# A one-core FFT filter with a maxout MLP: start-up work spread over ScalarE, GpSimd, VectorE and SyncE in another way

## The chip, the core and the metric

The kernel runs on one core of one Trainium2 chip. The metric is device microseconds of that core from the start to the end of one execution. The core has five engines that run side by side, each with its own instruction queue that is worked off in order: TensorE (PE in the profile; its weight loads are PEld), VectorE (DVE), ScalarE (ACT), GpSimd (POOL) and SyncE (SP), which here only issues DMAs. GpSimd issues DMAs too. Engines wait for each other through semaphores.

## What is computed

Per batch entry (8 of them, 3072 positions, 256 channels) a real FFT along the positions is multiplied by a filter and transformed back; every position then passes a maxout MLP.

```python
X = np.fft.rfft(x, axis=1)                       # x: (8, 3072, 256)
F = (filt_r + 1j * filt_i)[None, :, :]           # (1, 1537, 256)
y = np.fft.irfft(X * F, n=x.shape[1], axis=1)
h1, h2 = y @ w1, y @ w2                          # w1, w2: (256, 1024)
out = np.maximum(h1, h2) @ w_out                 # w_out: (1024, 256)
```

Inputs and output are float32; the kernel multiplies in bfloat16.

## The kernel before, in words

**Transforms as matmuls.** 3072 is split into 96 x 32. S1 (`s1t`, L507, for batch entry 0) multiplies x, 96 rows at a time, by the 96 x 96 sine and cosine table C1; x comes in eight chunks c of four m each. Its two results per chunk (dc = 0, 1) are evicted from PSUM to `at2` by ScalarE, or by VectorE where L514 says so. `t1` (L519) transposes `at2` into `bt`, in six parts. S2 (`s2`, L383) multiplies `bt` by the table U, the filter products `pq` (`product`, L392) come from VectorE and GpSimd, S3 (`s3t`, L530) goes back with the tables VP and VQ, which are U transposed on TensorE (`table_v`, `put_v`), and S4 (`s4`, L434) ends the transform with G1. The MLP (`moe_h`, L454, and `moe_o`, L475) uses max(h1, h2) = h2 + max(h1 - h2, 0): it needs Wd = w1 - w2 (`prep_wd`, on GpSimd, four parts), M = w2 w_out (`prep_t`, `prep_m`) and Wo = w_out. Batch entries 1 to 7 go through other functions (`f1`, `s1`, `visit`), which a plan interleaves with the MLP of the entry before; that part is long and is not touched.

**The tables** are computed at the start. C1 (`table_c`, L184): arguments on VectorE, then a sine on ScalarE, for which it loads its sine table (`ACT_TABLE_LOAD`). U (`tables_u`, L208): small columns on VectorE, four rows `t2` on ScalarE (L231), then for each half h the arguments `ua` on VectorE (L240 to L251), and a sine per half (`sines_u`).

**x of entry 0.** Chunks 0 and 1 are loaded as float32 by SyncE (L93) and cast to bfloat16 by ScalarE (`cast_x0`, L96); chunks 2 to 7 are loaded by GpSimd's DMAs, which cast on the way (L88). TensorE takes the chunks in the order 0, 2, 1, 3, 4, 5, 6, 7, with two matmuls on constants (`spin`) between them.

**The filter.** `load_f` (L119) brings the filter with GpSimd's DMAs, first half h = 0 (frequencies w 0 to 7), then h = 1 (w 8 to 11), each with g = 0, 1 (partitions 0 to 31 and 64 to 95) and real and imaginary part: four quarters per half, each of two or three DMAs. `double_f` (L135) copies a quarter to the 32 partitions behind it: half 0 by VectorE (L139), half 1 by SyncE's DMA (L141). `fix_f` mends one row.

**Order.** The program is written in the order in which each engine gets its work (manual schedule). On GpSimd: loads of x and small tables, `load_f`, four products, `prep_wd` with the loads of entry 1's x (L88) and of Wo (L300) between its parts. On SyncE: chunks 0 and 1, one filter row, the doublings of half 1, then w1 and w2 (L293, L294). On VectorE: the arguments of C1 and U, the S1 evictions of c = 6, 7, then by turns doublings and `bt` copies, then products. A DMA on either queue reuses one of eight semaphores, so it waits until the eighth before it has landed.

Of the kernel before, what the change touches and what calls it, by code (L numbers as in the profile page):

```python
# [17 lines left out]
NP = 96  # L18
# [8 lines left out]
def kernel(  # L27
# [55 lines left out]
    def load_x(b, c, n):  # L83
        for k in range(c, c + n):
            xb[b, k] = x_tile(b, k)[0:NP]
        src = x[b].rearrange("(p m) d -> p m d", m=NM)
        m0 = 4 * (c % 2)
        G.dma_start(out=xb[b][0:NP, m0:m0 + 4 * n], in_=src[:, 4 * c:4 * c + 4 * n, :])  # L88
# [4 lines left out]
        nc.sync.dma_start(out=XF[c][0:NP].rearrange("p a b d -> p (a b) d"),  # L93
                          in_=x[0].rearrange("(p m) d -> p m d", m=NM)[:, 4 * c:4 * c + 4, :])

    def cast_x0(c):  # L96
        S.activation(xb[0, c], XF[c][0:NP].rearrange("p a b d -> p (a b) d"), AF.Copy)  # L97

    def load_xf(b, c):
        src = x[b].rearrange("(h p m) d -> p h m d", h=2, m=NM)  # L100
# [34 lines left out]
    def double_f(h, g, ri, engine):  # L135
        w0, w1 = WP[h]
        o_, i_ = F[64 * g + 32:64 * g + 64, ri, w0:w1], F[64 * g:64 * g + 32, ri, w0:w1]
        if engine is V:
            V.tensor_copy(o_, i_)  # L139
        else:  # L140
            nc.sync.dma_start(out=o_, in_=i_)  # L141
# [31 lines left out]
    G.iota(cid, pattern=[[1, 128]], base=0, channel_multiplier=0, allow_small_or_imprecise_dtypes=True)  # L173
    for c in range(5, 8):
        load_x(0, c, 1)
    for q in range(2):
        G.memset(hv[:, q], 1.0)
        for r in (0, 32):
            G.memset(hv[r:r + 1, q], 0.5 * (1 - q))
# [4 lines left out]
    def table_c():  # L184
        p96 = init.tile([128, 1], FP32)
        V.tensor_scalar(p96, pid, 1.0 / 96.0, None, OP.mult)
        uc = init.tile([NP, 48, 2], FP32)
        rc = init.tile([NP, 48, 2], FP32)
        kf = kc.rearrange("p w g s -> p (w g s)")
        V.tensor_scalar(uc[:, :, 0], kf, p96[0:NP], 0.25, OP.mult, OP.add)  # L190
        V.tensor_scalar(uc[:, :, 1], kf, p96[0:NP], None, OP.mult)
        V.tensor_scalar(uc[:, 0:1, 1], pid[0:NP], 0.5, 0.25, OP.mult, OP.add)
        V.tensor_scalar(rc, uc, RND, RND, OP.add, OP.subtract)
        V.tensor_tensor(uc, uc, rc, OP.subtract)
        cast_x0(0)
        S.activation(C1, uc.rearrange("p k r -> p (k r)"), AF.Sin, bias=zero[0:NP], scale=TWO_PI)
        cast_x0(1)

    def table_ct():
        G.memset(CT, 0.0)  # L200
# [7 lines left out]
    def tables_u():  # L208
        def col(name):
            return init.tile([128, 1], FP32, name=name)  # L210

        pr, pm, rr, mm, a_, b_, base, nbase = (col("col%d" % i) for i in range(8))
        V.tensor_scalar(pr, pid, 64.0, None, OP.is_ge)
        V.tensor_scalar(pm, pr, -64.0, pid, OP.mult, OP.add)
        V.tensor_scalar(rr, pm, 32.0, None, OP.is_ge)
        V.tensor_scalar(mm, rr, -32.0, pm, OP.mult, OP.add)
        V.tensor_scalar(a_, mm, 1.0 / 3072.0, None, OP.mult)
        V.tensor_scalar(b_, mm, 1.0 / 32.0, None, OP.mult)
        V.tensor_tensor(base, pr, a_, OP.mult)
        of = init.tile([128, 2, 2], FP32)  # L220
        os_ = init.tile([128, 2], FP32)
        for c in range(2):
            V.tensor_scalar(of[:, c, 0:1], rr, 0.25, 0.25 + 0.25 * c, OP.mult, OP.add)
            V.tensor_scalar(of[:, c, 1:2], rr, -0.25, 0.25 + 0.25 * c, OP.mult, OP.add)
        V.tensor_scalar(of[:, :, 1], of[:, :, 1], b_, None, OP.add)
        for c in range(2):
            V.tensor_scalar(os_[32:64, c:c + 1], mm[32:64], 1.0 / 64.0, 0.25 + 0.25 * c, OP.mult, OP.add)
        t2 = init.tile([128, 2, 2, 16], FP32)
        for c in range(2):
            for s in range(2):  # L230
                S.activation(t2[:, c, s], jb, AF.Identity, bias=of[:, c, s:s + 1], scale=b_)  # L231
        t1 = init.tile([128, 2, NU], FP32)
        V.tensor_scalar(t1[:, 0], kap.rearrange("p w g -> p (w g)"), a_, base, OP.mult, OP.add)
        V.tensor_scalar(t1[:, 1], t1[:, 0], -1.0, None, OP.mult)
        uv = ua.rearrange("p u c s j -> p u (c s j)")
        for h in range(2):
            us = slice(NW * h, NW * h + NW)
            for c in range(2):
                for s in range(2):
                    V.tensor_tensor(ua[:, us, c, s],  # L240
                                    t1[:, s, us].rearrange("p (u o) -> p u o", o=1).to_broadcast([128, NW, 16]),
                                    t2[:, c, s].rearrange("p (o j) -> p o j", o=1).to_broadcast([128, NW, 16]),
                                    OP.add)
            if h == 0:
                V.tensor_scalar(ua[0:32, 0, 1, 0, 0:1], mm[0:32], 0.5, 0.25, OP.mult, OP.add)
                for c in range(2):
                    V.tensor_scalar(ua[32:64, 0, c, 1], jb[32:64], b_[32:64], os_[32:64, c:c + 1], OP.mult, OP.add)
                V.memset(ua[0:32, 0, :, 1], 0.0)
                V.memset(ua[32:64, 0, :, 0], 0.0)
            V.tensor_scalar(ru, uv[:, us], RND, RND, OP.add, OP.subtract)  # L250
            V.tensor_tensor(uv[:, us], uv[:, us], ru, OP.subtract)  # L251

    def sines_u(h):
        uv = ua.rearrange("p u c s j -> p u (c s j)")
# [7 lines left out]
    def table_v(h, q):  # L262
        pool, tag = (pso, "po") if h else (ps, "ps")
        pv = [pool.tile([128, 6, 64], FP32, tag=tag, name="pv%d" % s) for s in range(2)]
        for i in range(6):
            for g in range(2):
                for s in range(2):
                    rows = slice(64 * s, 64 * s + 64)
                    u = 2 * (6 * h + i) + g
                    if q == 0:  # L270
                        TE.matmul(pv[s][64 * g:64 * g + 64, i], U[rows, u], I128[rows, rows], start=True, stop=True)
                    else:
                        TE.matmul(pv[s][64 * g:64 * g + 32, i], U[rows, u, 32:64], I128[rows, rows],
                                  start=True, stop=True)
                        TE.matmul(pv[s][64 * g + 32:64 * g + 64, i], U[rows, u, 0:32], NI[rows, rows],
                                  start=True, stop=True)
        return pv

    def put_v(h, q, pv):
        for s in range(2):  # L280
            i0 = 1 if h == 0 and s == 0 else 0
            tab = VQ if q else VP
            if i0:
                S.activation(tab[:, 0, 0], pv[0][:, 0], AF.Identity, bias=zero, scale=hv[:, q])
            S.activation(tab[:, 6 * h + i0:6 * h + 6, s], pv[s][:, i0:6], AF.Copy)  # L285
# [13 lines left out]
    def load_wo():  # L299
        G.dma_start(out=Wo, in_=moe_w_out.rearrange("(c p) j -> p c j", p=128))  # L300

    def prep_wd(h, engine):
        js = slice(256 * h, 256 * h + 256)
        engine.tensor_tensor(Wd[:, :, js], w1f[:, :, js], w2f[:, :, js], OP.subtract)
# [202 lines left out]
    def s1t(c):  # L507
        for dc in range(2):
            pa = ps.tile([128, 4, 96], FP32, tag="ps", name="pa")
            for m in range(4):  # L510
                TE.matmul(pa[:, m], xb[0, c][:, m, 128 * dc:128 * dc + 128], C1, start=True, stop=True)
            o_ = at2[:, dc].rearrange("p u q m -> p (u q) m")[:, :, 4 * c:4 * c + 4]
            i_ = pa.rearrange("p m q -> p q m")
            if dc == 1 and c >= 6:  # L514
                V.tensor_copy(o_, i_)
            else:
                S.activation(o_, i_, AF.Copy)

    def t1(n, engine):  # L519
        pb = ps.tile([128, 4, D], BF16, tag="ps", name="pb")  # L520
        for i in range(4):
            for dc in range(2):
                TE.transpose(pb[:, i, 128 * dc:128 * dc + 128],
                             at2[:, dc, 4 * n + i].rearrange("p q m -> p (q m)"), I128)
        if engine is S:
            S.activation(bt[0][:, 4 * n:4 * n + 4], pb, AF.Copy)  # L526
        else:
            V.tensor_copy(bt[0][:, 4 * n:4 * n + 4], pb)
# [45 lines left out]
    table_c()  # L574
    V.tensor_scalar(I128, cid, pid, None, OP.is_equal)
    V.tensor_scalar(NI, cid, pid, -1.0, OP.is_equal, OP.mult)
    tables_u()
    for g in range(2):
        for ri in range(2):
            double_f(1, g, ri, nc.sync)  # L580
# [9 lines left out]
    sines_u(0)  # L590
    bt[0] = bpool.tile([128, NU, D], BF16, tag="bt", name="bt")
    for n in range(6):
        if n % 2 == 0:
            double_f(0, n // 4, n // 2 % 2, V)
        if n == 0:
            fix_f()
        t1(n, S if n % 2 else V)
    put_v(0, 0, table_v(0, 0))
    double_f(0, 1, 1, V)
    xs = {}  # L600

    def stage_x(v):
# [40 lines left out]
        pqs[v] = products(v)  # L643
    for v in (4, 5):
        s3t(v, pqs[v])
    prep_wd(0, G)
    load_x(1, 2, 2)
    prep_wd(1, G)
    load_x(1, 4, 2)
    load_wo()  # L650
    prep_wd(2, G)
    load_x(1, 6, 2)
    prep_wd(3, G)
# [101 lines left out]
```

## Time and profile before

| | |
|---|---|
| three runs | 507.33, 507.25, 505.11 us; median 507.25 |
| the profiled execution | 506.41 us, span 504.6 us |
| busy: TensorE | 488.9 us, 97% of the span |
| busy: VectorE, ScalarE, GpSimd | 332.4, 311.4, 255.5 us |
| mean granted TensorE clock | 0.99 |

The profile has one execution, with the start of every instruction in us from the start of the span. A timeline row gives start, duration, engine, line of the kernel, operation, what is written from what, the shapes, the count of instructions put together in the row, and in square brackets how long the engine had stood idle and what released it. A chain row gives start, duration, and the engine and line that the end of the program hung on at that moment; "issue" is time in which nothing was waited for that the profile shows. The granted clock is the share of full speed at which TensorE was allowed to run.

### The profile page before, as it was taken

Reading aid. Unit: us, or ns where it says so; the run is one execution under the profiler, and the core shown is the slowest. Engines: PE = TensorE matmul, PEld = TensorE weight load, DVE = VectorE, ACT = ScalarE, POOL = GpSimd, SP = SyncE. Lnnn points to the kernel's source line nnn. Section 1 sums busy time; section 2 is a strip of 40 time slices with the busy share of each in tenths; the row PEclk is TensorE's granted clock in tenths of the full one; section 3 lists DMA queues with packets and bytes.
Section 4 is the critical chain, followed back from the end, with each engine's and each line's share of the span. In section 5 each row is a group of like instructions: output and inputs, shape, how many; then the busy total and the mean of one; then the engine's idle time right before and its main releaser. Section 6 shows DMA issues by size and latency. Waiting matters only on the chain.

```text
span 504.6 us, 13082 instructions
## 1 busy us (share of the span) xinstructions
PE 488.9 (97%) x5300; PEld 362.6 (72%) x5300; DVE 332.4 (66%) x518; ACT 311.4 (62%) x632; POOL 255.5 (51%) x338
## 2 busy tenths in 40 slices
PE   6688999999999999999999999999999999999997
PEld 3455767777777777777777777777777777777775
DVE  6976678557775687557764687557764687554443
ACT  7776377746774586547774676646774465544442
POOL 7694369566663855627654656538632221222220
PEclk8979999999999999999999999999999999999999
DMA  9969789996699658886789659796669336411112
GB/s 190 168 172 189 220 231 299 289 268 210 209 257 280 179 179 245 247 221 200 198 244 259 190 187 256 216 256 185 197 178 248 89 112 162 168 64 64 64 64 84
DMA packets 77966, 97.59 MB, mean 193 GB/s; under 512 B 8017, under 2 KB 54354, under 8 KB 77842
## 3 DMA queue, kind: packets, MB, share of 16 engines
q1 hardware_dynamic: 64866, 67.52, 50.1%
q0 software_dynamic: 13040, 29.24, 19.9%
q8 instruction: 41, 0.67, 0.6%
q14 instruction: 19, 0.16, 0.1%
HBM read 53.87 MB, written 47.19 MB: 200 GB/s over the span
## 4 chain that ended last, share of the span: by engine, by line
PE 88%; DMA 5%; ACT 3%; DVE 2%; POOL 1%; issue 1%; SPq 0%; ACTq 0%; DVEq 0%
PE po L488 33%; PE ph L460 32%; PE po L486 8%; PE pz L411 5%; PE py L440 4%; PE pa L361 2%; PE px L388 2%; DMA Wo<-in_moe_w_out_dram 2%; DMA bt<-ad 1%; DMA XF<-in_x_dram 1%; DMA ad<-at 0%; PE pr L561 0%; ACT bt L526 0%; DVE ua L240 0%; ACT xb L97 0%
## 5 line engine op out<-in xcount | busy, mean ns | idle before, releaser
L488 PE MATMUL po<-Wo,gt 128*128 128x256 bf16 x1536 | 261.0, 273 | 0.6 <-DMA Wo<-in_moe_w_out_dram 0.6
L464 ACT ACTIVATE gt<-ph 128x384 bf16<-128x384 f32 x321 | 157.0, 496 | 147.9 <-PE ph L460 147.3
L473 POOL DMA_DIRECT2D out_dram<-ot x186 | 102.6, 555 | 184.0 <-DVE ot L500 181.1
L488 PEld LDWEIGHTS <-gt 128*128 128x128 bf16 x1536 | 146.6, 98 | 66.5 <-issue 10.7
L462 DVE TENSOR_SCALAR gt<-ph 128x384 bf16<-128x384 f32 x191 | 104.9, 552 | 63.0 <-PE ph L460 61.1
L394 DVE TENSOR_TENSOR pq<-px,F 128x1024 bf16<-128x1024 f32 x91 | 107.1, 1219 | 24.8 <-PE px L388 24.2
L460 PEld LDWEIGHTS <-Wd 128*128 128x128 bf16 x1024 | 96.6, 98 | 12.0 <-issue 0.5
L112 POOL TENSOR_TENSOR xb<-XF 128x512 bf16<-128x512 f32 x48 | 61.2, 1276 | 45.7 <-DMA XF<-in_x_dram 23.6
L500 DVE COPY ot<-po 128x512 f32<-128x512 f32 x95 | 65.1, 685 | 25.3 <-PE po L488 24.1
L113 POOL TENSOR_TENSOR xb<-XF 128x512 bf16<-128x512 f32 x48 | 61.0, 1271 | 0.0
L365 ACT ACTIVATE at<-pa 128x512 bf16<-128x512 f32 x96 | 51.8, 610 | 1.4 <-PE pa L361 1.1
L415 ACT ACTIVATE zt<-pz 128x512 bf16<-128x512 f32 x84 | 45.6, 595 | 11.5 <-PE pz L411 9.2
L440 PE MATMUL py<-G,zr 96*128 96x96 bf16 x512 | 32.7, 206 | 0.2
L440 PEld LDWEIGHTS <-zr 96*128 96x128 bf16 x512 | 28.9, 97 | 2.8 <-DVE zr L564 0.9
L388 PE MATMUL px<-bt,U 64*64 64x256 bf16 x384 | 20.2, 277 | 2.3 <-ACT VQ L285 1.0
L411 PE MATMUL pz<-pq,VP 64*64 64x256 bf16 x336 | 21.9, 281 | 0.0
L411 PE MATMUL pz<-pq,VQ 64*64 64x256 bf16 x336 | 20.9, 269 | 0.0
L361 PE MATMUL pa<-xb,CT 64*64 64x512 bf16 x192 | 19.5, 383 | 0.0
L411 PEld LDWEIGHTS <-VP 64*64 64x64 bf16 x336 | 9.7, 105 | 13.3 <-issue 13.3
L388 PEld LDWEIGHTS <-U 64*64 64x64 bf16 x384 | 10.4, 108 | 5.6 <-issue 4.5
L571 PE MATMUL pd<-W 128*128 128x512 bf16 x28 | 10.5, 479 | 1.5 <-DVE zero L154 1.5
L394 POOL TENSOR_TENSOR pq<-xs,F 128x1024 bf16<-128x1024 f32 x4 | 8.5, 2132 | 5.1 <-ACT VQ L285 4.0
(431 smaller groups left out, 609.6 us busy)
## 6 DMA issues: line engine op xcount, KB each, us to landing
out_dram<-ot POOLq DMA_DIRECT2D x186, 128.0 KB, 3.4
XF<-in_x_dram SPq DMA_DIRECT2D x96, 192.0 KB, 4.7
ad<-at SPq DMA_DIRECT2D x56, 192.0 KB, 4.0
bt<-ad SPq DMA_DIRECT2D x14, 768.0 KB, 8.9
zd<-zt SPq DMA_DIRECT2D x42, 256.0 KB, 2.4
zr<-zd SPq DMA_DIRECT2D x56, 192.0 KB, 4.9
WS<-in_moe_w_dram SPq DMA_DIRECT2D x4, 512.0 KB, 5.5
xb<-in_x_dram POOLq DMA_DIRECT2D x4, 384.0 KB, 8.3
```

The source lines that it names most:

```text
L112: G.tensor_tensor(t_[:, 0], f[:, 0], f[:, 1], OP.add)
L113: G.tensor_tensor(t_[:, 1], f[:, 0], f[:, 1], OP.subtract)
L365: S.activation(at[:, m0:m0 + 2], pa[g], AF.Copy)
L394: E.tensor_tensor(pq, px.rearrange("p (o i) d -> p o i d", o=1).to_broadcast([128, 2, 2, D]), F[:, :, 2 * v:2 * v + 2, s], OP.mult)
L411: TE.matmul(pz[g][64 * s:64 * s + 64, i], tab[64 * g:64 * g + 64, 2 * v + i, s], pq[s][64 * g:64 * g + 64, q, i], start=(q == 0), stop=(q ...
L440: TE.matmul(py[:, m], zr[b][:, 4 * i + m, 128 * dc:128 * dc + 128], G1, start=True, stop=True)
L460: TE.matmul(ph, Wd[:, dc, 128 * j:128 * j + 128], y_[:, dc], start=(dc == 0), stop=(dc == 1))
L462: V.tensor_scalar(gt[tt][:, j], ph, 0.0, None, OP.max)
L464: S.activation(gt[tt][:, j], ph, AF.Relu)
L473: E.dma_start(out=dst, in_=ot[tt // 2][:, 3 * (tt % 2) + c])
L488: TE.matmul(p_, g_[:, n - 2, blk], Wo[:, n - 2], start=(e == 0), stop=(e == 9))
L500: V.tensor_copy(ot[tt // 2][:, e - 1:e + 1], po[0])
```

## The change

- `table_c` takes the sine of C1 ahead of the casts of x; ScalarE casts chunk 0 after it, GpSimd chunk 1, behind its loads of x and ahead of `load_f`.
- S1's second result is evicted by VectorE for c = 3 to 7, not only for 6 and 7: five evictions on VectorE, eleven on ScalarE.
- The arguments of U's second half move behind VectorE's last `bt` copy.
- Of half 0 of the filter, the two quarters of g = 1 are doubled by SyncE, at the head of its doublings; the two of g = 0 stay on VectorE, before the `bt` copies 0 and 2, with `fix_f` after the second.
- On GpSimd, entry 1's chunks 2 and 3 are loaded ahead of the first `prep_wd`; chunks 4 and 5 and Wo ahead of the second.

TensorE's instructions and their order stay as they are.

```diff
-    def cast_x0(c):
-        S.activation(xb[0, c], XF[c][0:NP].rearrange("p a b d -> p (a b) d"), AF.Copy)
+    def cast_x0(c, engine):
+        i_ = XF[c][0:NP].rearrange("p a b d -> p (a b) d")
+        if engine is S:
+            S.activation(xb[0, c], i_, AF.Copy)
+        else:
+            engine.tensor_copy(xb[0, c], i_)
...
     for c in range(5, 8):
         load_x(0, c, 1)
+    cast_x0(1, G)
...
         V.tensor_tensor(uc, uc, rc, OP.subtract)
-        cast_x0(0)
         S.activation(C1, uc.rearrange("p k r -> p (k r)"), AF.Sin, bias=zero[0:NP], scale=TWO_PI)
-        cast_x0(1)
+        cast_x0(0, S)
...
-        for h in range(2):
+        def args(h):
...
             V.tensor_scalar(ru, uv[:, us], RND, RND, OP.add, OP.subtract)
             V.tensor_tensor(uv[:, us], uv[:, us], ru, OP.subtract)
+
+        args(0)
+        return args
...
-            if dc == 1 and c >= 6:
+            if dc == 1 and c >= 3:
                 V.tensor_copy(o_, i_)
...
-    tables_u()
+    args = tables_u()
+    for ri in range(2):
+        double_f(0, 1, ri, nc.sync)
     for g in range(2):
         for ri in range(2):
             double_f(1, g, ri, nc.sync)
...
     for n in range(6):
-        if n % 2 == 0:
-            double_f(0, n // 4, n // 2 % 2, V)
-        if n == 0:
+        if n < 4 and n % 2 == 0:
+            double_f(0, 0, n // 2, V)
+        if n == 2:
             fix_f()
         t1(n, S if n % 2 else V)
+    args(1)
     put_v(0, 0, table_v(0, 0))
-    double_f(0, 1, 1, V)
...
+    load_x(1, 2, 2)
     prep_wd(0, G)
-    load_x(1, 2, 2)
-    prep_wd(1, G)
     load_x(1, 4, 2)
     load_wo()
+    prep_wd(1, G)
     prep_wd(2, G)
```

## The prediction

> **What bounds the kernel now.** First the busy time by stage, in three windows; then the chain that ended last; then the rows of single engines in the first 32 us. In the windows a line gives the window, its length, and the busy time (with instruction count) of TensorE, its weight loads, VectorE, ScalarE and GpSimd, then the granted clock.
>
> ```profile
> 0.00:50.00 50.00, 38.22 (x618) 23.18 (x619) 37.33 (x80) 36.92 (x70) 34.41 (x56) 0.90 0.92 178
> 20.00:32.00 12.00, 7.96 (x230) 4.54 (x233) 10.40 (x10) 7.81 (x17) 7.19 (x5) 0.72 0.88 247
> 50.00:504.60 454.60, 450.70 (x4685) 339.46 (x4682) 295.05 (x438) 274.51 (x562) 221.10 (x282) 1.00 0.68 195
> ```
>
> From 50 us on TensorE is busy 450.70 of 454.60 us: that stage ends when its matmuls are done, and the diff leaves its instructions alone. The first 50 us leave TensorE idle for 50 - 38.22 = 11.78 us, 4.04 of them between 20 and 32. All the edits lie there, so the change is worth what it moves the start of the steady stage. The chain of waits (start, duration, what) says through whom:
>
> ```profile
> 4.70 1.06 ACT xb L97
> ...
> 25.08 0.83 ACT U L255
> ...
> 28.05 0.97 PE pt L534 x2
> 29.02 1.01 PE pt L540 x24
> ...
> 31.68 1.97 POOL pq L394
> ...
> 36.66 1.28 POOL Wd L304
> 37.95 0.46 POOL xb L88
> 38.41 10.63 DMA Wo<-in_moe_w_out_dram
> 49.08 0.60 PE po L488 x4
> ```
>
> From the cast of the first x chunk the chain runs through S1, the transposes, a stretch in which TensorE and ScalarE hand small tables to each other, a GpSimd product, GpSimd's queue, and the load of Wo, for which the first output matmul waits until 49.08. The reader is to see that a step which is late anywhere up to 38 us is late at 50 us too.
>
> **The change part by part.** *Table load and casts.* ScalarE's timeline, 5.77 to 14.75 us:
>
> ```profile
> 5.77 1.28 ACT L196 ACT_TABLE_LOAD   x1
> 7.07 0.37 ACT L196 ACTIVATE C<-uc,zero 96x96 bf16<-96x96 f32 x1
> 7.35 1.04 ACT L97 ACTIVATE xb<-XF 96x1024 bf16<-96x1024 f32 x1
> 8.29 1.25 ACT L231 ACTIVATE t<-jb,of,col 128x16 f32<-128x16 f32 x4
> 9.45 1.59 ACT L517 ACTIVATE at<-pa 128x384 bf16<-128x384 f32 x4
> 10.93 0.24 ACT L260 ACTIVATE G<-pg 96x96 bf16<-96x96 f32 x1
> 11.06 3.69 ACT L517 ACTIVATE at<-pa 128x384 bf16<-128x384 f32 x9
> ```
>
> The order of instructions in the changed kernel has one table load left on ScalarE, ahead of C1; C1 is then done while x is still on its way. The cast of chunk 0 still ends at 4.70 + 1.06 = 5.76, and now S1 can start there, not at 7.07 + 0.37 = 7.44: 1.7 us sooner. ScalarE's next work, the four t rows, needs the "of" columns of VectorE:
>
> ```profile
> 6.18 0.23 DVE L225 TENSOR_SCALAR of<-of,col 128x2 f32<-128x2 f32 x1
> ```
>
> They exist at 6.41, so t takes 6.45 to 7.70 (1.25), and the first S1 eviction moves from 9.45 to 7.70. Of the evictions 11 stay on ScalarE at 3.69 / 9 = 0.41, with G1's 0.24: 4.75 us, to 12.45. Two more rows, of GpSimd and of TensorE:
>
> ```profile
> 11.95 0.57 POOL L129 DMA_DIRECT2D F<-in_filt_r_dram  x1 [0.52 <-DMA xb<-in_x_dram]
> ```
> ```profile
> 14.66 0.51 PE L511 MATMUL pa<-C,xb 96*128 96x96 bf16 x8
> ```
>
> The data allow no more: chunk 7 lands at 11.95 (the wait in the first of them ends with an x load, by the order of the queue the last one), its matmuls take 0.51 (the second row), its eviction 0.41: 12.9.
>
> *VectorE.* Its timeline from the second half of the arguments on:
>
> ```profile
> 12.24 1.16 DVE L240 TENSOR_TENSOR ua<-t,t 128x192 f32<-128x192 f32 x4
> 13.43 0.56 DVE L250 TENSOR_SCALAR ru<-ua 128x768 f32<-128x768 f32 x1
> 14.03 0.96 DVE L251 TENSOR_TENSOR ua<-ua,ru 128x768 f32<-128x768 f32 x1
> 14.90 1.01 DVE L515 CAST at<-pa 128x384 bf16<-128x384 f32 x2
> 15.95 1.34 DVE L139 COPY F<-F 32x4096 bf16<-32x4096 bf16 x1
> 17.32 0.28 DVE L149 CAST F<-FN 1x256 bf16<-1x256 f32 x1
> 17.64 0.69 DVE L528 COPY bt<-pb 128x1024 bf16<-128x1024 bf16 x1
> ```
>
> The first half of the arguments ends at 12.3; it hangs on t, which comes 1.75 sooner: 10.6. Then come five evictions at 1.01 / 2 = 0.5, to 13.1; the last of them waits for chunk 7 (12.45 + 0.5 = 13.0), the same. So S1 is out at 13.1, against 14.90 + 1.01 = 15.9: **2.8 us sooner**. ScalarE's bt copies, and the table hand-over behind them, follow S1: 2.8 sooner as well.
>
> VectorE itself goes on with the first doubling, which needs a filter quarter. This row's wait ends with a filter load:
>
> ```profile
> 13.58 0.57 POOL L129 DMA_DIRECT2D F<-in_filt_i_dram  x1 [0.32 <-DMA F<-in_filt_r_dram]
> ```
>
> By the queue's order it is the second of three pieces of that quarter; I take 14.1 for the third, a small one. From there: two doublings (1.34 each), three bt copies (0.69 each), the fix (0.28), and the second half of the arguments (12.24 to 14.99 = 2.75): 2.68 + 2.07 + 0.28 + 2.75 = 7.8, to 21.9. Its products start now at 24.03, and then at 22.0:
>
> ```profile
> 24.03 5.75 DVE L394 TENSOR_TENSOR pq<-px,F 128x1024 bf16<-128x1024 f32 x5 [0.51 <-DVE F L139]
> ```
>
> Two doublings, 2.7 us, left VectorE here, 2.75 us of arguments came in: no gain by itself; the gain is that the arguments no longer stand ahead of S1's last evictions. The second sine (U, at 25.08 in the chain) wants its arguments at about 25.08 - 2.8 = 22.3, so 21.9 is in time by 0.4; what comes later than that counts.
>
> *The doublings on SyncE* add a wait: the first product now waits for two DMAs. They hang on the filter load issued at 13.58; behind them in SyncE's queue stand the other four doublings, which wait for later loads anyway, and then the loads of w1 and w2. The DMAs that write the filter tile, up to 30 us, from issue to landing:
>
> ```profile
> DMA to landing us min/median/max: 2.3/4.7/6.3
> ```
>
> The least belongs to the present doublings by DMA, the median to a load. 13.58 + 4.7, and 0.6 for the issue as in the row at 13.58, is 18.9; a doubling of twice the size lands between 2.3 (size costs nothing) and 4.6 (it costs all) later: 21.2 to 23.5. I take 21.8, near the row; the upper end would cost 1.5 us.
>
> *The GpSimd cast* of chunk 1 isn't in the trace. Bounds: ScalarE's 1.04 for the same cast, and this two-input product of the same length:
>
> ```profile
> L394 POOL TENSOR_TENSOR pq<-xs,F 128x1024 bf16<-128x1024 f32 x4 | 8.5, 2132 | 5.1 <-ACT VQ L285 4.0 <-ACT xs L604 1.1
> ```
>
> I take 1.3, nearer the cast. It starts at about 5.8, when the chunk has landed, and ends between 6.8 and 7.9; TensorE takes chunk 1 third, at about 8. All filter loads are issued 1.3 later, but the wait at 11.95 shows them behind the x loads, so up to 2.1 is hidden by transfers still to come. The GPSIMD Engine Reference of the Trainium skill (section 4.1) calls one-input work roughly line-rate; an estimate from its 1.03 cycles per element at 1.2 GHz (section 3.1) is 0.9 us; no row here shows it, and the sum would stay as it is.
>
> *The sum.* Product v=4 needs its px, whose matmuls run at 29.92, right after VectorE's five products end (24.03 + 5.75 = 29.78):
>
> ```profile
> 29.92 0.64 PE L388 MATMUL px<-bt,U 64*64 64x256 bf16 x8
> ```
>
> With products from 22.0 they end at 27.75. ScalarE's side would allow 2.8, VectorE's allows 2.0: the later one decides, and GpSimd's product at 31.68 moves to 29.7. Behind it GpSimd's queue is reordered: one Wd part less (1.28) stands ahead of Wo, so Wo lands 1.28 sooner still, and the wait for it goes:
>
> ```profile
> L488 PE MATMUL po<-Wo,gt 128*128 128x256 bf16 x1536 | 261.0, 273 | 0.6 <-DMA Wo<-in_moe_w_out_dram 0.6
> ```
>
> I count 0.5 of its 0.6, because TensorE then meets the w2T copy. The Wd parts that come later are still ahead of the first maxout step that reads them. Together **2.0 + 0.5 = 2.5 us**. The profiled execution took 506.41 us (span 504.6, and 1.8 around it), which gives 503.9. The median of the three runs, 507.25, is 0.84 higher; one execution can't say which is typical, so I put half of that back: **504.3 us**.
>
> **The rivals.** *1. GpSimd's cast holds VectorE.*
>
> ```profile
> 16.23 1.16 POOL L126 DMA_DIRECT2D F<-in_filt_r_dram  x1
> ```
>
> The two engines hinder each other here: this DMA issue on GpSimd, beside the doubling at 15.95, took 1.16, against 0.57 at 13.58. If VectorE stands while the cast runs (5.8 to between 6.8 and 7.9), "of" comes 1.0 to 2.1 later, and with it t, the arguments and S1: out at 14.1 to 15.2. The chain then gains 1.8 to 0.7 in place of 2.0, so 504.5 to 505.6. Against it: VectorE's small operations may not need what the cast holds. SBUF — State Buffer in the Trainium skill ("SBUF: two separate sides") calls the port pair that both engines share an exclusive lock, held for a whole instruction; the row above fits, for DMA issues only.
>
> *2. The filters come late, and the kernel is slower.* Place: the first product's wait for SyncE's doublings. If the cast takes 2.13 and delays the filter loads in full, and doubling costs by size and the load lands after the slowest time of the filter tile's DMAs, the product starts at 13.58 + 2.13 + 6.3 + 0.6 + 4.6 = 27.2, 3.2 later than now; less 0.5 for Wo it is 2.7 slower: 509.5. It decides from 24.5 on. Against it: four costs at their upper ends at once.
>
> *3 and 4. TensorE's clock.* From 20 to 32 us the granted clock is 0.72, and the two chain pieces at 28.05 and 29.02 (1.98 us) run in its low part. Where the low stretch falls in the changed kernel I can't derive. If it misses these pieces, about 1.0 more is won: 503.3. If it reaches on over the later S3 pieces, about 1.5 is lost: 505.8.
>
> **How the numbers follow.** Forecast 504.3 with 0.48 (its own range 503.4 to 505.2); VectorE held 0.14; clock worse 0.16; clock better 0.10; filters late 0.12. A measurement of this kernel can tell about 0.5% from no change, which is 504.7 to 509.8. Faster: 0.33 of the forecast, the better clock's 0.10, 0.04 of rival 1: 0.47. Slower: 0.07 of the late filters, whose 509.5 is near the edge. Same: the rest, 0.46. Range: from the better clock with the forecast's width below it, 502.2, to the worse clock with the doublings at their upper end, 505.8 + 1.5 = 507.3; that leaves out the late filters and some of the edges.
>
> **What would show it.** S1's first matmul at 5.8 and its last eviction near 13.1; no table load after the first; ScalarE's first eviction at 7.7 (8.8 or later: rival 1); the first product at 22.0, waiting for nothing or for a doubling (after 24.5: rival 2); VectorE's arguments done before the second sine; the px of v=4 near 27.9; Wo issued 3.3 us sooner than 38.41, with no TensorE wait for it; from there on the same matmuls to the end. It is wrong if the stage from 16 to 32 us doesn't move with S1, or if the later start of the steady stage is made up by waits after 50 us.

## The result, and the profile after

Over 22 runs of each, the changed kernel has a median of 505.0 us (504.05 to 507.23) and the kernel before 506.85 us (505.11 to 508.71). The ratio is **0.9965, 95% interval [0.9953, 0.9976]**: 1.8 us or 0.35% less. That is inside the 0.5% that the prediction called no change. The profiled execution took 505.85 us, span 504.1.

The three windows of the changed kernel (window, length, busy time of TensorE, weight loads, VectorE, ScalarE, GpSimd, then the granted clock):

```profile
0.00:50.00 50.00, 39.15 (x626) 23.70 (x627) 37.12 (x81) 34.16 (x65) 35.33 (x57) 0.90 1.00 198
20.00:32.00 12.00, 7.99 (x236) 4.38 (x229) 10.99 (x15) 8.59 (x20) 7.74 (x6) 0.72 0.87 213
50.00:504.10 454.10, 449.98 (x4676) 338.66 (x4674) 295.24 (x438) 274.39 (x562) 221.09 (x282) 1.00 0.69 194
```

TensorE does 0.93 us more of its work in the first 50 us (39.15 against 38.22); from 20 to 32 us nothing has changed, 7.99 against 7.96. So the stage in which the prediction had put most of the gain looks as before. ScalarE's timeline shows why, from the first t row to the end of S1:

```profile
7.32 0.98 ACT L235 ACTIVATE t<-jb,of,col 128x16 f32<-128x16 f32 x3 [0.85 <-DVE of L229]
8.20 1.60 ACT L524 ACTIVATE at<-pa 128x384 bf16<-128x384 f32 x4
9.68 0.24 ACT L267 ACTIVATE G<-pg 96x96 bf16<-96x96 f32 x1
10.09 0.87 ACT L524 ACTIVATE at<-pa 128x384 bf16<-128x384 f32 x2 [0.16 <-PE pa L518]
11.58 0.49 ACT L524 ACTIVATE at<-pa 128x384 bf16<-128x384 f32 x1 [0.62 <-PE pa L518]
12.72 0.49 ACT L524 ACTIVATE at<-pa 128x384 bf16<-128x384 f32 x1 [0.65 <-PE pa L518]
```

The first eviction came at 8.20 (9.45 before), 1.25 sooner. But before, the rows at 9.45 and 11.06 ran without a gap: ScalarE always had a result of TensorE to evict. Now it stands before nearly every eviction and waits for TensorE (0.16, 0.62, 0.65). TensorE's own timeline, the first row a wait, the others the chunks with the filling matmuls (`pd`) between them:

```profile
8.72 1.01 PE L578 MATMUL pd<-W 128*128 128x512 bf16 x2 [1.39 <-ACT at L524]
9.52 0.85 PE L518 MATMUL pa<-C,xb 96*128 96x96 bf16 x8
10.17 1.05 PE L578 MATMUL pd<-W 128*128 128x512 bf16 x2
11.02 0.85 PE L518 MATMUL pa<-C,xb 96*128 96x96 bf16 x8
...
13.90 0.50 PE L518 MATMUL pa<-C,xb 96*128 96x96 bf16 x8
14.24 0.60 PE L578 MATMUL pd<-W 128*128 128x512 bf16 x2
14.67 0.51 PE L518 MATMUL pa<-C,xb 96*128 96x96 bf16 x8
```

From chunk to chunk it takes 11.02 - 9.52 = 1.50 us in the low clock and 14.67 - 13.90 = 0.77 in the full one. The last chunk starts at 14.67, where it started at 14.66 before: the whole head start of 1.6 us is gone at the end of S1. It went in the wait of 1.39 us for ScalarE's first eviction, and in the low clock behind it (granted 0.50 until about 12.2 us here, until about 11.2 before). VectorE's last eviction and what it does next:

```profile
15.21 0.56 DVE L522 CAST at<-pa 128x384 bf16<-128x384 f32 x1 [0.22 <-PE pa L518]
15.80 1.22 DVE L143 COPY F<-F 32x4096 bf16<-32x4096 bf16 x1
...
22.45 0.96 DVE L255 TENSOR_TENSOR ua<-ua,ru 128x768 f32<-128x768 f32 x1
24.32 3.49 DVE L401 TENSOR_TENSOR pq<-px,F 128x1024 bf16<-128x1024 f32 x3 [0.91 <-DMA F<-in_filt_i_dram]
```

S1 ends at 15.21 + 0.56 = 15.77, against 15.91. The arguments end at 23.41, and then VectorE waits 0.91 for the filter tile. The row names a filter load; GpSimd, which reads the same tile and starts 0.04 later, names SyncE's doubling:

```profile
24.36 2.12 POOL L401 TENSOR_TENSOR pq<-xs,F 128x1024 bf16<-128x1024 f32 x1 [4.25 <-DMA F<-F]
```

The issue row of those doublings, and their time to landing (least, median, most):

```profile
L145 SPq DMA_DIRECT2D F<-F x6: 507/520/858, 17.1 to 24.6; - x6
...
DMA to landing us min/median/max: 2.6/4.3/5.7
```

What remains of the gain lies behind 36 us. GpSimd issues Wo at 36.71 in place of 38.41, and no output matmul waits for it:

```profile
36.71 0.93 POOL L307 DMA_DIRECT2D Wo<-in_moe_w_out_dram  x1
```
```profile
L495 PE MATMUL po<-Wo,gt 128*128 128x256 bf16 x1536 | 261.0, 273 | 0.0
```

The chain shows that the first output matmul now comes from VectorE's casts of w2 (`w2b`) and the transposes behind them, at 48.32 in place of 49.08:

```profile
46.82 0.34 DVE w2b L304
47.21 0.56 PE pt L318 x7
47.77 0.22 PE pa L343
47.99 0.33 PE ph L467 x2
48.32 0.44 PE po L495 x4
```

From this profile alone the gain would be GpSimd's new order and nothing else. That was the first theory, and the experiments threw it over.

### The profile page after: what moved, and what is told of

It is laid out like the page before. It is cut to its first block, busy times and chain, and to the rows that moved or that the text cites. A ratio compares the mean times of both kernels' runs of the same rounds, so it can differ in the third digit from the quotient of the medians.

```text
span 504.1 us, 13082 instructions
## 1 busy us (share of the span) xinstructions
PE 489.1 (97%) x5300; PEld 362.4 (72%) x5300; DVE 332.4 (66%) x519; ACT 308.6 (61%) x627; POOL 256.4 (51%) x339
## 4 chain that ended last, share of the span: by engine, by line
PE 93%; ACT 3%; DVE 2%; issue 1%; POOL 1%; POOLq 0%
PE po L495 34%; PE ph L467 33%; PE po L493 8%; PE pz L418 5%; PE py L447 4%; PE pa L368 2%; PE px L395 2%; PE pd L578 1%; PE pt L547 1%; PE pr L568 1%; PE pa L518 0%; DVE at L346 0%; PE pt L541 0%; ACT bt L533 0%; DVE gt L469 0%
```

## The experiments

All were run in five rounds beside the kernel before, on one chip per group; ratios are to the kernel before of the same group.

**1. GpSimd's order alone** (on the kernel before):

```diff
+    load_x(1, 2, 2)
     prep_wd(0, G)
-    load_x(1, 2, 2)
-    prep_wd(1, G)
     load_x(1, 4, 2)
     load_wo()
+    prep_wd(1, G)
```

> The kernel before with only GpSimd's new order behind its products (x of the next batch, one Wd part, x, Wo, then the other Wd parts). Theory (the whole gain comes from this order, through Wo that lands earlier): as good as the changed kernel, 0.2 to 0.5% faster than before; Wo issued about 1.3 us sooner than 38.41, no TensorE wait for Wo, and a later wait for px or bt near 65 us shorter; everything up to 33 us as before. Rival (the gain comes from the front: table first, casts moved): ratio 1.000, within 0.1%, with the wait for Wo merely turned into the wait for w2b or w2T.

Measured: 506.03 us, ratio 0.9984 [0.9972, 0.9996]. About half of the gain, not all, though the intervals just touch. Its first output matmul too waits for nothing, but later TensorE waits 1.02 for `bt` of the next entry, where it waited 0.22 before:

```profile
66.27 0.41 PE L388 MATMUL px<-bt,U 64*64 64x256 bf16 x8 [1.02 <-DMA bt<-ad]
```

**2. GpSimd's order undone** (the diff of 1, backwards, on the changed kernel):

> The changed kernel with GpSimd's old order behind its products. Theory (the order is the gain): ratio to before 0.999 to 1.001; first output matmul waits for Wo again. Rival (the front is the gain, because px of v=4 came 0.5 us sooner in the changed kernel's trace): half or more of the 0.35% stays, ratio 0.9965 to 0.998.

Measured: 505.48 us, ratio 0.9982 [0.9963, 1.0002], too wide to decide between the two by itself. Its trace is worth more: it has the changed kernel's S1, and here the granted clock stayed at 1.00 from 8 to 16 us (0.79 in the changed kernel's trace). VectorE's rows at the end of S1 and at the first product:

```profile
13.92 0.56 DVE L522 CAST at<-pa 128x384 bf16<-128x384 f32 x1 [0.22 <-PE pa L518]
...
23.02 4.62 DVE L401 TENSOR_TENSOR pq<-px,F 128x1024 bf16<-128x1024 f32 x4 [0.90 <-DMA F<-in_filt_i_dram]
```

S1 ends at 14.48, 1.29 sooner than with the low clock, and the products start 1.30 sooner, still behind a filter wait of 0.9. So one profiled execution had told of the front in a bad case. Nor does the first output matmul of this trace wait for Wo, against the theory: it starts at 46.38, although Wo keeps its old place in GpSimd's queue.

**3. Chunk 1 cast by ScalarE** (on the changed kernel):

```diff
-    cast_x0(1, G)
...
         cast_x0(0, S)
+        cast_x0(1, S)
```

> The changed kernel with chunk 1 cast on ScalarE behind chunk 0, and nothing on GpSimd. Theory of the hold: the 128x2 operation of VectorE that took 1.10 us beside GpSimd's cast takes 0.2 to 0.3 again, although its place in VectorE's order is the same. ScalarE's t comes at about 6.9 (it now stands behind the second cast), the first eviction of S1 at 7.6 to 8.0 in place of 8.20. S1's end stays within 0.3 us of 15.77, since TensorE sets it; time within 0.1% of the changed kernel, ratio to before 0.9955 to 0.9975. Rival (the hold is something else, such as a wait for the columns from ScalarE): the operation still takes about 1.1.

Measured: 504.62 us, ratio 0.9958 [0.9945, 0.9972], as the changed kernel within what can be told. The hold is GpSimd's cast. First the two rows of the changed kernel, then the same operation here:

```profile
6.18 1.10 DVE L229 TENSOR_SCALAR of<-of,col 128x2 f32<-128x2 f32 x1
```
```profile
6.19 1.03 POOL L101 CAST xb<-XF 96x1024 bf16<-96x1024 f32 x1 [0.50 <-DMA XF<-in_x_dram]
```
```profile
6.19 0.23 DVE L229 TENSOR_SCALAR of<-of,col 128x2 f32<-128x2 f32 x1
```

0.23 without the cast, 1.10 beside it, until the cast is over at 7.22. What the hold costs, this run can't tell: the first eviction comes at 8.14 here (7.6 to 8.0 was expected) and at 8.20 there, since ScalarE's second cast takes the place of the wait. The trace of experiment 6 tells more. There the chunk landed later and GpSimd's cast began at 6.31 in place of 6.19; the 128x2 operation, begun at 6.17, took 0.23, and the first eviction came at 7.33. So 0.12 us in the start of the cast decided over 0.87 us at the first eviction.

**4. No filling matmuls in S1** (on the changed kernel; they compute nothing that is used):

```diff
-        if c < 7:
-            spin(2)
```

> The changed kernel without the two filling matmuls between the chunks of S1 (they compute nothing that is used; the nine ahead of S1 stay). Theory (TensorE sets S1's end from 8.7 us on: two fillers and eight matmuls per chunk): S1's last eviction ends at 13 to 14.5 in place of 15.77, ScalarE's and VectorE's evictions then set the pace; but the first product still waits for SyncE's doublings at about 24, so px of v=4 does not move by more than 0.4 and the time by no more than 0.1% from the changed kernel. Rival a (S1's end is what counts): px of v=4 1 to 2 us sooner, ratio to before 0.992 to 0.995. Rival b (without the fillers the clock is granted later or is worse in the next stage): slower than the changed kernel by 0.1 to 0.4%.

Measured: 505.93 us, ratio 0.9978 [0.9966, 0.9989]: 0.13% behind the changed kernel's ratio, which is the way of rival b, but the intervals overlap. S1 does end sooner, VectorE's last eviction at 11.81 + 1.94 = 13.75 against 15.77, so TensorE did set its end. But the clock pays for it (the column behind the five busy times):

```profile
8.00:16.00 8.00, 6.40 (x66) 5.61 (x66) 7.74 (x19) 5.80 (x15) 7.28 (x13) 0.59 1.17 191
16.00:20.00 4.00, 3.47 (x53) 3.18 (x51) 3.73 (x8) 2.63 (x4) 3.60 (x6) 0.55 1.04 195
```

0.59 and 0.55, where the changed kernel's trace has 0.79 and 1.00; over all its runs the mean granted clock was 0.978 to 0.986, against 0.986 to 0.993. The second sine of U came at 24.90, later than the 24.55 of the changed kernel. TensorE: Matmul & The Clock Gate in the Trainium skill ("What's actually happening") says that activity releases the throttle and that it is judged in a free-running window of some 3.4 us. The rows agree: less TensorE work, less clock; and in the changed kernel's trace, which grants 0.50 from 9 to 12 us, 0.79 over 8 us comes to (1 - 0.79) x 8 / 0.5 = 3.4 us of low clock, present in one execution of the same S1 and absent in the next.

**5. All four quarters doubled by VectorE** (on the changed kernel):

```diff
-    for ri in range(2):
-        double_f(0, 1, ri, nc.sync)
...
-        if n < 4 and n % 2 == 0:
-            double_f(0, 0, n // 2, V)
-        if n == 2:
+        if n % 2 == 0:
+            double_f(0, n // 4, n // 2 % 2, V)
+        if n == 0:
             fix_f()
...
+    double_f(0, 1, 1, V)
```

> The changed kernel, with all four quarters of the first filter half doubled on VectorE in the places that the kernel before has, and nothing else undone. Theory (the two doublings on SyncE let the first product start as early as VectorE's other work allows, though they land late): VectorE has two doublings of 1.2 more and ends its arguments at about 24.6, so that GpSimd's and VectorE's first products come at 25 to 26 in place of 24.3; 1 to 1.5 us slower than the changed kernel, ratio to before 0.9985 to 1.001. Rival (moving them is worth nothing, because they land as late as VectorE would have done them): as the changed kernel, 0.9955 to 0.9975.

Measured: 505.04 us, ratio 0.9968 [0.9951, 0.9984]; the rival. The first product came at 24.61, without a wait, where the changed kernel has it at 24.32 behind a wait. But S1 had the full clock here; against experiment 2, where it had too, the first product is 1.6 us later (24.61 against 23.02), as the theory has it, and the time is the same all the same. So by these runs the two doublings may stand on either engine, and the time does not follow the start of the first product.

**6. The front alone** (the kernel before with these lines of the change, and no other):

```diff
     for c in range(5, 8):
         load_x(0, c, 1)
+    cast_x0(1, G)
...
-        cast_x0(0)
         S.activation(C1, uc.rearrange("p k r -> p (k r)"), AF.Sin, bias=zero[0:NP], scale=TWO_PI)
-        cast_x0(1)
+        cast_x0(0, S)
```

> The kernel before with the front alone: sine table ahead of the casts, chunk 0 cast by ScalarE and chunk 1 by GpSimd; evictions, arguments, doublings and GpSimd's order as before. Theory (S1's later chunks are paced by TensorE, two filling and eight computing matmuls per chunk, and by the half clock, so an early start is lost): first matmul of S1 at 5.9 in place of 7.5, end of S1 within 0.4 us of 15.9, ratio 0.998 to 1.000. Rival (the half of the gain that remained without GpSimd's new order comes from the front): 0.9965 to 0.998, S1's end 0.7 us or more sooner.

Measured: 505.0 us, ratio **0.9955 [0.9933, 0.9977]**: these lines alone give what the whole change gives. That is the rival, and more than its range; the theory that GpSimd's order is the whole gain does not survive it. ScalarE's S1 and VectorE's last evictions here:

```profile
7.33 1.60 ACT L521 ACTIVATE at<-pa 128x384 bf16<-128x384 f32 x4
8.80 0.24 ACT L264 ACTIVATE G<-pg 96x96 bf16<-96x96 f32 x1
8.94 3.66 ACT L521 ACTIVATE at<-pa 128x384 bf16<-128x384 f32 x9
```
```profile
12.78 0.96 DVE L255 TENSOR_TENSOR ua<-ua,ru 128x768 f32<-128x768 f32 x1
13.66 1.01 DVE L519 CAST at<-pa 128x384 bf16<-128x384 f32 x2
```

ScalarE evicts without a gap again, from 7.33 (9.45 before), and S1 ends at 14.67 (15.91), 1.24 sooner, with VectorE's arguments as the last to be done. The arguments hang on ScalarE's t, which starts at 6.06 in place of 8.29, now that no table load and no second cast stand ahead of it; they end at 12.78 + 0.96 = 13.74 in place of 14.99, and this 1.25 is the gain at the end of S1. The clock was full from 8 to 16 us here (0.80 in the kernel before's trace); how this kernel's S1 does in the low clock, no trace shows. Over the first 50 us the mean granted clock is 0.90 in both traces, and the first output matmul starts at 47.08 in place of 49.08. It does not wait for Wo any more, although Wo keeps its old place in GpSimd's queue; by a hair, since Wo, issued at 37.26, takes 9.8 us to land:

```profile
47.08 0.60 PE L492 MATMUL po<-Wo,gt 128*128 128x256 bf16 x4
```

**7. The second row group of the filter loaded first** (on the changed kernel):

```diff
-        for g in range(2):
+        for g in ((1, 0) if h == 0 else (0, 1)):
```

> The changed kernel with the loads of the second row group of the first filter half issued ahead of those of the first group, so that SyncE's two doublings find their data sooner and VectorE's two later. Theory (GpSimd's products, back to back from 24.36 because they wait for SyncE's doublings, hold TensorE by 0.88 us in the stage behind): doublings issued at 14 to 15.5 in place of 17.06, landed by 20 to 22.5 in place of 24.2; first products at 22.5 to 23.5, TensorE's wait for GpSimd's product gone; 0.4 to 1.0 us faster than the changed kernel, ratio to before 0.9945 to 0.996. Rival (VectorE's doublings then come late and push the arguments, or the chain of ScalarE and TensorE sets the end anyway): as the changed kernel or slower, 0.9965 to 0.999.

Measured: 509.1 us, ratio **1.0041 [1.0026, 1.0056]**, 3.9 us slower than the changed kernel by the ratios (0.0076 x 506.9), which neither forecast had. SyncE's doublings were indeed early; GpSimd's first product started at 21.81 in place of 24.36. But VectorE:

```profile
17.03 1.22 DVE L143 COPY F<-F 32x4096 bf16<-32x4096 bf16 x1 [1.45 <-DMA F<-in_filt_r_dram]
...
21.87 5.01 DVE L244 TENSOR_TENSOR ua<-t,t 128x192 f32<-128x192 f32 x4
```

Its doubling waited 1.45 for the other group, as the rival has it; that is the small part. The four additions of the arguments, 1.17 in the changed kernel, took 5.01: they ran beside GpSimd's products of 21.81 and 24.55, 2.12 us each. The second sine came at 28.50 in place of 24.55. This was a new cause, and experiments 10 and 12 went after it.

**8. One filling matmul in place of two** (on the changed kernel): `spin(1)` for `spin(2)`.

> The changed kernel with one filling matmul between the chunks of S1 in place of two. Theory (TensorE paces S1, and the filling matmuls hold the granted clock up): S1's last eviction ends at 14.3 to 15.2 in place of 15.77; if the mean granted clock stays between 0.986 and 0.993, the time is 0.5 to 1.2 us below the changed kernel's, ratio 0.994 to 0.996. Rival (any filling matmul less gives clock away as no filling matmul at all did, 0.978 to 0.986): ratio 0.9965 to 0.9985.

Measured: 505.29 us, ratio 0.9963 [0.9943, 0.9983]. The ratio lies between the two forecasts, with an interval that reaches into both. S1 ended at 13.48 in its trace, at full clock, 1.0 sooner than in experiment 2; not by the filling matmul alone, since the hold of experiment 3 fell on another operation here too, and the first eviction came at 7.33 in place of 8.19. The first products still came at 24.25. So a whole microsecond at the end of S1 brought nothing that can be told: the filter, for which GpSimd's first product waits there too, did not come sooner with it.

```profile
24.29 2.12 POOL L401 TENSOR_TENSOR pq<-xs,F 128x1024 bf16<-128x1024 f32 x1 [4.46 <-DMA F<-F]
```

**9. Front and GpSimd's order** (the diffs of 6 and 1 together):

> The kernel before with the front (sine table ahead of the casts, chunk 0 cast by ScalarE, chunk 1 by GpSimd) and GpSimd's new order, but with S1's evictions, the arguments and the doublings as before. Theory (front and order are the gain, 0.45% and 0.16% alone; the other three edits give nothing): as good as the changed kernel or better, ratio to before 0.993 to 0.9965, S1's end near 14.7 with VectorE's arguments the last wait, first product near 22.7. Rival (the later arguments and the evictions on VectorE are needed to use the earlier start): 0.997 to 0.999.

Measured: 504.67 us, ratio 0.9971 [0.996, 0.9983]. As good as the whole change within the intervals, and no better than the front alone: in the traces with the front there is no wait for Wo left that the order could remove. The ratio itself falls into the rival's range, by 0.0001, and its interval reaches into both, so this run does not decide between them.

**10. Only one quarter doubled by SyncE** (on the changed kernel):

```diff
-    for ri in range(2):
-        double_f(0, 1, ri, nc.sync)
+    double_f(0, 1, 0, nc.sync)
...
-        if n < 4 and n % 2 == 0:
-            double_f(0, 0, n // 2, V)
+        if n % 2 == 0:
+            double_f(0, n // 4, (0, 1, 1)[n // 2], V)
```

> The changed kernel with one of the two doublings given back to VectorE (the last loaded quarter), so that SyncE doubles only the third quarter. Theory (the second SyncE doubling, landing at 22.6 to 24.2 in every trace that has it, sets the first product): the one SyncE doubling lands at 19.5 to 22.8, VectorE ends its arguments about 1.2 later than in the changed kernel, and the first products come at 22.5 to 24.6, the spread being the clock's in S1; ratio to before 0.9945 to 0.997, that is 0 to 0.7 us better than the changed kernel. Rival (the first product is not on the path, the chain of ScalarE and TensorE is): ratio as the changed kernel within 0.1%, whatever the first product does.

Measured: 507.8 us, ratio **1.0026 [1.0011, 1.0041]**; both theories missed. GpSimd's products and VectorE's arguments, and the sine that waits for them:

```profile
20.88 2.17 POOL L401 TENSOR_TENSOR pq<-xs,F 128x1024 bf16<-128x1024 f32 x1
...
23.59 2.13 POOL L401 TENSOR_TENSOR pq<-xs,F 128x1024 bf16<-128x1024 f32 x1
```
```profile
20.44 3.09 DVE L244 TENSOR_TENSOR ua<-t,t 128x192 f32<-128x192 f32 x4
23.56 2.58 DVE L254 TENSOR_SCALAR ru<-ua 128x768 f32<-128x768 f32 x1
26.18 0.96 DVE L255 TENSOR_TENSOR ua<-ua,ru 128x768 f32<-128x768 f32 x1
```
```profile
27.18 0.94 ACT L262 ACTIVATE U<-ua,zero 128x768 bf16<-128x768 f32 x1 [3.73 <-DVE ua L255]
```

1.17 became 3.09 and 0.56 became 2.58: each time nearly one GpSimd product was added. ScalarE stood 3.73 us. In the changed kernel GpSimd's products start at 24.36, 0.95 behind the arguments: the late doublings keep the two engines apart.

**11. The other three edits alone** (the changed kernel with the diffs of 6 and 1 undone):

> The kernel before with only the other three edits: more evictions on VectorE, later arguments, two quarters doubled by SyncE; table, casts and GpSimd's order as before. Theory (these three give nothing without the front, and little with it): ratio 0.999 to 1.002; S1's end 15 to 16, first product at 24 to 25 waiting for a doubling. Rival (they take evictions from ScalarE, which paces S1 in the kernel before without a gap): S1's end 1 us or more sooner, ratio 0.9965 to 0.998.

Measured: 507.17 us, ratio 1.0015 [0.9997, 1.0034]. More evictions on VectorE, later arguments and doublings on SyncE gain nothing by themselves. The first product stood at 24.36 behind a doubling, and TensorE paced the end of S1 (ScalarE waits 0.28 before each of its last three evictions). Whether the three cost something beside the front is not shown: experiment 2, which is the front with these three, has 0.9982 against 0.9955 for the front alone, but the intervals overlap.

**12. One quarter on SyncE, arguments early** (on kernel 9):

```diff
+    double_f(0, 1, 0, nc.sync)
...
-            double_f(0, n // 4, n // 2 % 2, V)
+            double_f(0, n // 4, (0, 1, 1)[n // 2], V)
...
-    double_f(0, 1, 1, V)
```

> The kernel before with the front and GpSimd's new order, and with the third quarter doubled by SyncE; the arguments and the evictions stay as before, so that all arguments are done before GpSimd's first product can start. Theory (one SyncE doubling made the kernel slower with late arguments only because GpSimd's product then ran beside VectorE's arguments and held them, three operations of 0.3 to 0.6 becoming 2 to 2.6): the argument operations take 0.3, 0.56 and 0.96 again and end near 13.7, the second sine is not late (23 to 24), first products at 21.5 to 23; ratio to before 0.993 to 0.9975, that is about 2.5 us below the kernel with late arguments and one SyncE doubling. Rival (the SyncE doubling itself, by its transfer, is what made that kernel slow): the second sine at 25 or later, or TensorE waiting for filters; ratio 1.000 to 1.004.

Measured: 505.0 us, ratio **0.9963 [0.9949, 0.9976]**, 0.63% or 3.2 us below kernel 10, with the same doubling on SyncE. The arguments:

```profile
11.02 1.16 DVE L244 TENSOR_TENSOR ua<-t,t 128x192 f32<-128x192 f32 x4
12.21 0.56 DVE L254 TENSOR_SCALAR ru<-ua 128x768 f32<-128x768 f32 x1
12.80 0.96 DVE L255 TENSOR_TENSOR ua<-ua,ru 128x768 f32<-128x768 f32 x1
```

1.16 and 0.56 again, and the second sine at 23.88. This kernel also has the evictions of the kernel before, so the time alone is not one edit's; the durations of the operations are. No version beat the changed kernel by more than the intervals: 3, 5, 6, 8, 9 and 12 lie between 0.9955 and 0.9971.

## Why the prediction was right, and where it was not

The range held the time (505.0 in 502.2 to 507.3), and the forecast missed by 0.7 us. The sign was right, the likeliest class, faster by over 0.5%, was not: 0.35%. And the sum was put together from steps of which several failed. Of its 2.5 us, 2.0 were to come through VectorE's products, which started 0.3 later than before (24.32 against 24.03). That the forecast still came near is in part luck. (The lower end of the range, by its own terms, is 503.3 - 0.9 = 502.4 and not 502.2; nothing hangs on it.)

- **The front** was right. The sine first puts S1's first matmul at 5.87 (predicted 5.8), with no second table load. Alone it is the gain (experiment 6), there through ScalarE's t and VectorE's arguments.
- **S1's end** is the step that failed: "S1 is out at 13.1, against 15.9: 2.8 us sooner". The trace has 15.77, and 14.48 with full clock. I had reckoned evictions and the landing of chunk 7, and of TensorE only the last chunk's 0.51. Two things were not in the sum. After two chunks TensorE waits for ScalarE's first eviction (1.39, and 1.28 in experiment 2). And it has a pace per chunk, two filling matmuls and eight others, of 0.77 at full and 1.50 at low clock, which stands in TensorE's rows; from 8.71 on, at full clock, this puts the last chunk of experiment 2 at 13.38. So the rebalancing could win little: with the last chunk at 14.66 or 14.67, S1 ends at 15.91 behind the arguments in the kernel before and at 15.77 without them in the changed one.
- **Rival 1**, GpSimd's cast holds VectorE, came true: "of" was 0.9 late and ScalarE's t with it. Its price, 0.2 to 1.3 us (a gain of 1.8 to 0.7 in place of 2.0), no run gives: experiment 3 is as fast without the hold, but has a cast more on ScalarE; the traces give 0.87 us at the first eviction, and not what becomes of it. SBUF — State Buffer in the Trainium skill ("SBUF: two separate sides") describes the port pair as an exclusive lock; 1.10 against 0.23 agrees, and so does the bigger case of experiments 7 and 10, that I had not thought of.
- **The first product** was predicted at 22.0 and came at 24.32. "The least belongs to the present doublings by DMA", and 21.8 for the landing with 23.5 as the upper end: the two doublings were issued at 17.06 and 18.6, sooner than the 18.9 that I had, but took 5.7 and 5.6 us to land in place of 2.3 to 4.6, so that even the upper end was too early. (In experiment 2 they took 3.8 and 4.4.) Rival 2's place was the right one, its price (slower from 24.5 on) was not reached by 0.2; and a later start of the products at the same clock is partly a shield, as experiments 7 and 10 show.
- **"No gain by itself"** for the exchange of two doublings against arguments on VectorE was right (experiments 5 and 11). What the step lacked is that the arguments so moved come near GpSimd's products.
- **px of v=4** was to move from 29.92 to 27.9; it came at 29.40.
- **Wo**: issued 1.70 sooner, not 3.3, and its wait is gone as predicted. But the 0.5 is no term of its own beside the front: in its trace the front alone removes the same wait (6), and front with order (9) is no better than the front.
- **The clock**: 0.72 from 20 to 32 us in both traces. The stretch that mattered was another, 8 to 16 us, in which the same S1 had 0.79 in one execution and 1.00 in the next, 1.29 us apart. The times on record say how much of the gain this is. Of the kernel before's executions in the groups of the experiments, 53 of 112 had a mean granted clock of 0.989 or more, with a median of 506.32 us; of the changed kernel's, 18 of 22, with 504.93. So at like clock about 1.4 us of the 1.8 are left; the rest goes with the low clock, which came more rarely. With the front alone all 12 executions had 0.989 or more, but with experiment 12, which has the front too, 6 of 11; what brings the low clock is not shown.

What stays open: why the low clock came more rarely; and whether the small losses between px and the steady stage in kernel 8, for which the end of S1 moved and the time did not, have one cause.

## What to carry to other kernels

Before taking work from the engine that ends a stage last, work out the pace of the next slowest at the clock that it may get; where that is near, as TensorE was behind VectorE's arguments here, the rebalancing is worth next to nothing. Keep VectorE's operations on SBUF alone away from GpSimd's: a transfer that lands sooner can start GpSimd beside them and cost more than it gave. And try the parts of a change one by one, since here the move of one sine and one cast was the gain, and three edits gave nothing that could be told.

## What the runs showed of the hardware

- A GpSimd operation holds some VectorE operations until it is over: 128x2 from 0.23 to 1.10 beside a cast of 1.03; 128x768 from 0.56 to 2.58 beside a product of 2.13. Not all: VectorE's products from PSUM took 5.75 / 5 = 1.15 beside GpSimd's products in the kernel before. In experiment 6 the cast ran from 6.31 to 7.34, and of VectorE's operations there the two of 32x1 kept their time and the 128x24 one (0.30 to 0.33 elsewhere) did not:

```profile
6.31 1.03 POOL L101 CAST xb<-XF 96x1024 bf16<-96x1024 f32 x1 [0.61 <-DMA XF<-in_x_dram]
```
```profile
6.43 0.20 DVE L231 TENSOR_SCALAR os__191<-col 32x1 f32<-32x1 f32 x2
6.65 0.76 DVE L237 TENSOR_SCALAR t<-kap,col,col 128x24 f32<-128x24 f32 x1
```

- Less TensorE work gave less TensorE clock: 0.59 in place of 0.79 from 8 to 16 us without the filling matmuls, and 0.978 to 0.986 in place of 0.986 to 0.993 over the whole run; with one in place of two it was 0.985 to 0.992.
- A doubling of 256 KB within SBUF by DMA took 5.6 to 5.7 us to land in the changed kernel and 3.1 to 6.7 in the other traces; one of 128 KB took 2.3 to 2.4 in the kernel before, and 3.6 in the median in the changed one.
